# Longer load runs for k and v, 32-row products, and fewer whole-batch stores in a fused attention and spectral-mixing kernel

## The chip, the cores and the metric

One core of one Trainium2 chip. In the profile lines PE is the tensor engine (PEld its weight loads), DVE the vector engine, ACT the scalar engine, POOL the engine that issues the loads; PSUM is where this kernel's matmuls put their results. The metric is the device time of one execution in microseconds (us); lower is better. The kernel before has a median of 425.81 us (4 runs with the first measurement).

## The reference, cut to what matters

```python
# q, k, v: (8 batches, 8 heads, 576 rows, 64), float32
q_p, k_p = phi(q), phi(k)                       # phi(x) = elu(x) + 1
kv  = einsum('bhsd,bhse->bhde', k_p, v)         # per head: 64 x 64, summed over the 576 rows
z   = sum(k_p, axis=2)
x   = einsum('bhsd,bhde->bhse', q_p, kv) / (einsum('bhsd,bhd->bhs', q_p, z) + 1e-6)
# then, on x as (8, 576, 512): rfft over the rows, 64 modes, each times its own complex
# 512 x 512 weight (w_r, w_i: 134 MB in float32), irfft, u = x + y, out = u + relu(u @ w_ch)
```

The sum over s in `kv` does not care in which order the rows stand, as long as k and v have the same order. The change uses that.

## The kernel before

k and v of one batch are loaded so that a partition holds 9 consecutive rows (2,304 bytes of HBM, 1,152 bytes once cast to 16 bits). A head then fills 64 partitions. q has 18 rows to a partition.

```python
rows_in = src[b].rearrange("h s d -> (h s) d").rearrange(
    "(hp r j) d -> r hp (j d)", r=128, j=2 * NJ if nm == "q" else NJ)      # NJ = 9
...
shape = [128, 2, 2 * NJ * Dh] if nm == "q" else [128, NHP, NJ * Dh]
t = sA.tile(shape, F16, tag=f"{nm}16", bufs=2, name=f"{nm}16_{b}")
pin(nc.gpsimd.dma_start(out=t, in_=rows_in))
```

The products of k and v contract 64 rows; the two halves of the array (h2) alternate. Their sum is copied out by ACT (`kv`). Multiplied with q it gives the numerators of x, `num` below:

```python
def sum_kv(b):
    kv_ps = psA.tile([128, 2, 512], F32, tag="big", bufs=3, name=f"kvp{b}")
    for hpp in range(2):
        for j in range(NJ):
            for h2 in range(2):
                nc.tensor.matmul(kv_ps[:, h2, hpp*130 : hpp*130+130],
                                 phi["k", b][HALVES[h2], hpp, j]..., vp[HALVES[h2], hpp::2, j, 0:65], ...)
    # ... two ACT copies of 64 x 260 into kv_all[b]
```

Per batch the attention phase then runs, in this order (cut):

```python
turn_q(b, 0); turn_q(b, 1); sum_kv(b)      # tiles of tag "big", 3 buffers
features(b + 1)                            # DVE
exps(b + 2)                                # ACT: 4 passes
for jj in range(5):
    form_x(b, jj)                          # numerators `num`: one tile "big" each; jj = 4 is the tail
    if b > 1 and jj == 1: place_x(b - 2)   # `xp`: one tile "big", copied out by DVE and ACT into xt_c
    ...                                    # transforms of batch b - 1
```

`turn_q` transposes q (`qTp`), and `place_x` lays a batch's transformed rows out for the mode products (`xp`, copied out as `xt_c`).

Then 32 pairs of modes stream their weights (`w`, two transfers of 1 MB written per pair, two resident buffers), and at the end the output is stored. A batch in `QUADS` is stored whole (8 KB runs); the others in halves (4 KB runs):

```python
QUADS = (2, 4, 5, 6)
...
if t0 < B * NJJ and t0 // NJJ in QUADS:
    if t0 % NJJ:
        store(t0 - 2, NJJ)
    return
store(t0, 2)
```

## Time and profile before

| | before |
|---|---|
| span of the profiled execution | 422.9 us |
| load queue busy, from the packet records | 5.2 to 389.5 us |
| first products of the first mode pair | 113.9 us |
| last store issued / last store packet ends | 415.6 / 421.5 us |

From the page (busy time; then the 40 slices of the span in tenths; then packets by size):

```profile
PE 279.6 (66%) x3426; PEld 153.2 (36%) x3426; DVE 215.4 (51%) x446; ACT 161.7 (38%) x253; POOL 56.5 (13%) x99
...
DMA  9999999999999999999999999999999999996797
...
DMA packets 20227, 93.20 MB, mean 220 GB/s; under 512 B 2016, under 2 KB 11104, under 8 KB 15520
```

No compute engine is over 66% busy, and the DMA engines are full from the first slice to the thirty-sixth. The kernel is bound by its load stream. Compute matters in only two ways: if it is so late that the load queue runs dry, and after the last weight.

The store phase, by stretches (busy us of each engine, then granted clock, DMA share, GB/s):

```profile
396.00:400.00 4.00, 4.00 (x22) 1.22 (x21) 3.70 (x4) 3.38 (x8) 0.00 (x0) 1.00 1.00 383
400.00:404.00 4.00, 4.00 (x27) 1.11 (x27) 3.92 (x4) 3.46 (x7) 0.00 (x0) 1.00 0.79 321
404.00:408.00 4.00, 4.00 (x22) 0.82 (x20) 4.00 (x4) 3.47 (x8) 0.00 (x0) 1.00 0.99 388
408.00:412.00 4.00, 4.00 (x25) 1.17 (x24) 3.97 (x5) 3.63 (x7) 0.00 (x0) 1.00 1.04 431
```

The DMA share falls to 0.79 in one stretch: in the packet records fewer than 12 of 16 engines have a packet from 400.96 to 402.01 us. The stores wait there for the whole of batch 2.

The first mode pair, in order of time:

```profile
113.94 1.95 PE L442 MATMUL P<-w,xt_c 64*32 64x512 bf16 x32 [1.40 <-ACT xt_c L350]
```

### The profile page before, as it was taken

What the parts mean: (1) busy time and instruction counts of PE and PEld (TensorE: products, weight loads), DVE (VectorE), ACT (ScalarE), POOL (GpSimd) and SP (SyncE); (2) the same over time, 40 slices, a digit from 0 to 9 for tenths busy, and PEclk for the clock granted to TensorE, in tenths of its full rate; (3) what the DMA queues carried; (4) which work ended last, traced back from release to release, by engine and by line L of the source; (5) the groups of instructions that cost most, each with busy time, mean ns of one, the idle gap of its engine ahead of it and who ended that gap; (6) DMA issues with size and microseconds to landing.
All of it is one profiled execution on the core that took longest, in us unless ns stands there. A gap on an engine that the chain in (4) does not pass through costs nothing.

```text
span 422.9 us, 7976 instructions
## 1 busy us (share of the span) xinstructions
PE 279.6 (66%) x3426; PEld 153.2 (36%) x3426; DVE 215.4 (51%) x446; ACT 161.7 (38%) x253; POOL 56.5 (13%) x99
## 2 busy tenths in 40 slices
PE   1358387788717645344344768878798886989991
PEld 0246366666402322222122333334243333465320
DVE  4599488886202453354444434454264333423892
ACT  4688578754201102000000234444254351331881
POOL 4222124210000111111011111110110001130000
PEclk9999778869855555555555598999799896899997
DMA  9999999999999999999999999999999999996797
GB/s 217 210 208 215 207 220 202 224 209 222 221 215 219 207 215 217 222 211 217 218 212 217 217 220 214 215 216 215 214 219 220 215 212 219 223 201 126 248 409 287
DMA packets 20227, 93.20 MB, mean 220 GB/s; under 512 B 2016, under 2 KB 11104, under 8 KB 15520
## 3 DMA queue, kind: packets, MB, share of 16 engines
q0 software_dynamic: 16512, 81.47, 94.0%
q1 hardware_dynamic: 3680, 11.22, 7.0%
q8 instruction: 27, 0.44, 0.4%
q14 instruction: 8, 0.07, 0.0%
HBM read 163.93 MB, written 9.44 MB: 410 GB/s over the span
## 4 chain that ended last, share of the span: by engine, by line
DMA 63%; PE 22%; DVE 4%; ACT 3%; issue 2%; POOL 2%; DVEq 0%; POOLq 0%; ACTq 0%
DMA w<-in_moe_w_i_dram 48%; DMA pick_sb<-row_pick 8%; PE P L442 7%; DMA k<-in_k_dram 7%; PE acc L736 3%; PE acc L775 2%; PE zl L425 2%; ACT ke L213 2%; POOL w L119 1%; PE eps L677 1%; DVE ys L452 1%; PE ya L654 1%; PE yt L460 1%; PE xTp L667 1%; PE z L699 1%
## 5 line engine op out<-in xcount | busy, mean ns | idle before, releaser
L442 PE MATMUL P<-w,xt_c 64*32 64x512 bf16 (+2 forms) x1000 | 50.2, 531 | 59.7 <-DMA w<-in_moe_w_i_dram 58.3
L452 DVE CAST ys<-P 128x512 f16<-128x512 f32 x32 | 22.1, 692 | 122.2 <-PE P L442 122.2
L454 ACT CAST ys<-P 128x512 f16<-128x512 f32 x31 | 18.1, 585 | 154.1 <-PE P L442 154.1
L119 POOL DMA_DIRECT2D w<-in_moe_w_r_dram x31 | 16.6, 534 | 246.2 <-PE P L442 96.4
L442 PEld LDWEIGHTS <-xt_c 64*32 64x32 bf16 (+2 forms) x1000 | 16.7, 127 | 79.8 <-DMA w<-in_moe_w_i_dram 44.6
L165 PEld LDWEIGHTS <-qT 64*128 64x128 f16 (+1 forms) x640 | 23.0, 123 | 49.8 <-issue 31.0
L677 PE MATMUL eps<-wch,xTw 128*128 128x512 f16 x144 | 40.2, 406 | 0.0
L165 PE MATMUL num<-kv,qT 64*128 64x65 f16 (+1 forms) x320 | 13.7, 209 | 25.4 <-ACT xt_c L350 12.0
L658 DVE TENSOR_TENSOR x_main<-ya,x_main 128x512 f32<-128x512 f32 x32 | 22.0, 689 | 13.4 <-PE ya L654 13.2
L660 ACT CAST x16w<-x_main 128x512 f16<-128x512 f32 x32 | 19.8, 618 | 23.4 <-DVE x_main L658 22.3
L165 PE MATMUL nw<-kv,qT 64*128 64x65 f16 (+1 forms) x320 | 19.0, 240 | 9.5 <-DVE x_tail L621 4.3
L685 ACT CAST E<-eps 128x512 f16<-128x512 f32 (+1 forms) x40 | 21.2, 540 | 8.5 <-PE eps L677 8.4
L299 DVE TENSOR_TENSOR x<-num,rd 128x512 f16<-128x512 f32 x32 | 22.1, 692 | 1.1
L242 PE MATMUL qTp<-id,qe 128*128 128x128 f16 x144 | 16.1, 301 | 9.9 <-DVE qe L226 9.4
L460 PE MATMUL yt<-pick_sb,ys 128*128 128x16 f16 x252 | 11.7, 174 | 16.3 <-DMA pick_sb<-row_pick 9.6
L213 ACT ACTIVATE qe<-q 128x1152 f16<-128x1152 f16 (+1 forms) x16 | 17.9, 1157 | 10.4 <-DMA q<-in_q_dram 6.5
L249 ACT COPY qT<-qTp 128x1152 f16<-128x1152 f16 x16 | 19.6, 1287 | 0.7 <-PE qTp L242 0.2
L425 PE MATMUL zl<-wch,id 128*128 128x512 f16 x72 | 19.6, 408 | 0.0
L213 ACT ACTIVATE ke<-k 128x1152 f16<-128x1152 f16 x16 | 17.7, 1152 | 4.9 <-DMA k<-in_k_dram 4.9
L460 PEld LDWEIGHTS <-ys 128*128 128x128 f16 x252 | 9.7, 102 | 26.4 <-DVE ys L452 15.0
L785 ACT ACTIVATE acc<-acc 128x512 f32<-128x512 f32 x34 | 18.1, 582 | 2.4 <-PE acc L736 1.6
L242 PEld LDWEIGHTS <-qe 128*128 128x128 f16 x144 | 13.8, 140 | 11.0 <-DVE qe L226 9.8
(113 smaller groups left out, 468.6 us busy)
## 6 DMA issues: line engine op xcount, KB each, us to landing
w<-in_moe_w_r_dram POOLq DMA_DIRECT2D x31, 1024.0 KB, 12.5
w<-in_moe_w_i_dram POOLq DMA_DIRECT2D x31, 1024.0 KB, 17.0
k<-in_k_dram POOLq DMA_DIRECT2D x8, 576.0 KB, 12.8
v<-in_v_dram POOLq DMA_DIRECT2D x8, 576.0 KB, 14.8
out_dram<-x_main SPq DMA_DIRECT2D x4, 1024.0 KB, 4.9
q<-in_q_dram POOLq DMA_DIRECT2D x7, 576.0 KB, 12.9
out_dram<-x_main SPq DMA_DIRECT2D x6, 512.0 KB, 4.6
q<-in_q_dram SPq DMA_DIRECT2D x2, 576.0 KB, 4.3
```

What stands on the lines that cost most here:

```text
L119: nc.gpsimd.dma_start(out=w_in[p][half::2], in_=two.rearrange("g (r dc) e -> (g r) dc e", dc=NDW))
L165: mm = nc.tensor.matmul(num[hpo][orow, c0 : c0 + 65], qT[rows, hpp, h2, cols], kv_sb[rows, hpp, h2, :])
L213: pin(nc.scalar.activation(out=ev[:, c], in_=heads(nm, b, c), func=AF.Exp))
L242: nc.tensor.transpose(qT_ps[:, j], phi["q", b][:, c, j].rearrange("p o d -> p (o d)"), id16,)
L299: nc.vector.tensor_tensor(out=dst.rearrange("p (o c d) -> p o c d", o=2, c=4), in0=nv[:, :, :, 0:64], in1=rden.unsqueeze(3).broadcast_to([ ...
L425: pin(nc.tensor.matmul(last_ps[0], id16, wch16[:, 0, :]))
L442: nc.tensor.matmul(P[c : c + n, :], xt_cols(dc, kk, n), w[rows, dc, :], start=(dc < NDC), stop=(dc >= n_dc - NDC), tile_position=(rows.sta ...
L452: pin(nc.vector.tensor_copy(out=st, in_=P))
L460: nc.tensor.matmul(yt_ps[:, ec, kk % 8, :], st[:, ec * 128 : ec * 128 + 128], pick_sb)
L658: pin(nc.vector.tensor_tensor(out=x, in0=acc, in1=x, op=ALU.add))
L677: nc.tensor.matmul(e_ps, xT[:, c, :], wch16[:, c, :], start=(c == 0), stop=(c == NDC - 1))
L685: pin(nc.scalar.copy(out=dst, in_=e_ps[:, cols]))
```

## The change

Its intent: k and v in runs of 18 rows, so half as many packets, each twice as large. A head then fills only 32 partitions, so its products contract 32 rows, and there are twice as many of them. Besides, only batches 5 and 6 are stored whole.

```diff
-                "(hp r j) d -> r hp (j d)", r=128, j=2 * NJ if nm == "q" else NJ
+                "(hp r j) d -> r hp (j d)", r=128, j=2 * NJ
...
-        kv_ps = psA.tile([128, 2, 512], F32, tag="big", bufs=3, name=f"kvp{b}")
-        for hpp in range(2):
-            for j in range(NJ):
+        for pair in range(2):
+            kv_ps = psA.tile([128, 2, 512], F32, tag="big", bufs=3, name=f"kvp{b}_{pair}")
+            for j in range(2 * NJ):
                 for h2 in range(2):
+                    r0 = 64 * pair + 32 * h2
                     pin(
                         nc.tensor.matmul(
-                            kv_ps[:, h2, hpp * 130 : hpp * 130 + 130],
-                            phi["k", b][HALVES[h2], hpp, j].rearrange("p o d -> p (o d)"),
-                            vp[HALVES[h2], hpp::2, j, 0:65],
+                            kv_ps[:, h2, 0:130],
+                            phi["k", b][r0 : r0 + 32, j // NJ, j % NJ].rearrange("p o d -> p (o d)"),
+                            vp[r0 : r0 + 32, :, j, 0:65],
...
+                            tile_position=(r0, 0),
...              # the two ACT copies of 64 x 260 become four of 64 x 130
-    QUADS = (2, 4, 5, 6)
+    QUADS = (5, 6)
```

More of the change, by code (lines that the diff above doesn't have):

```diff
@@ L141 @@
     n_pre, n_keep = W_PRE, W_KEEP
-    vp = sA.tile([128, NHP, NJ, 66], F16, name="vpad")
+    vp = sA.tile([128, 2, 2 * NJ, 66], F16, name="vpad")
     nc.vector.memset(vp[:, :, :, 64:66], 1.0)
@@ L190, in load @@
                 continue
-            shape = [128, 2, 2 * NJ * Dh] if nm == "q" else [128, NHP, NJ * Dh]
-            t = sA.tile(shape, F16, tag=f"{nm}16", bufs=2, name=f"{nm}16_{b}")
+            t = sA.tile([128, 2, 2 * NJ * Dh], F16, tag=f"{nm}16", bufs=2, name=f"{nm}16_{b}")
             pin(nc.gpsimd.dma_start(out=t, in_=rows_in))
@@ L198, in heads @@
             return raw[nm, b, c].rearrange("p o (j d) -> p o j d", d=Dh)
-        if nm == "q":
-            return raw[nm, b].rearrange("p o (c j d) -> p c o j d", c=2, d=Dh)[:, c]
-        return raw[nm, b].rearrange("p (o c) (j d) -> p c o j d", o=2, d=Dh)[:, c]
+        return raw[nm, b].rearrange("p o (c j d) -> p c o j d", c=2, d=Dh)[:, c]
     def flat(nm, b):
@@ L254, in sum_kv @@
     def sum_kv(b):
-        kv_ps = psA.tile([128, 2, 512], F32, tag="big", bufs=3, name=f"kvp{b}")
-        for hpp in range(2):
-            for j in range(NJ):
+        for pair in range(2):
+            kv_ps = psA.tile([128, 2, 512], F32, tag="big", bufs=3, name=f"kvp{b}_{pair}")
+            for j in range(2 * NJ):
                 for h2 in range(2):
+                    r0 = 64 * pair + 32 * h2
                     pin(
                         nc.tensor.matmul(
-                            kv_ps[:, h2, hpp * 130 : hpp * 130 + 130],
-                            phi["k", b][HALVES[h2], hpp, j].rearrange("p o d -> p (o d)"),
-                            vp[HALVES[h2], hpp::2, j, 0:65],
+                            kv_ps[:, h2, 0:130],
+                            phi["k", b][r0 : r0 + 32, j // NJ, j % NJ].rearrange("p o d -> p (o d)"),
+                            vp[r0 : r0 + 32, :, j, 0:65],
                             start=(j == 0),
-                            stop=(j == NJ - 1),
-                        )
-                    )
-        for hpo in range(2):
-            rows = HALVES[hpo]
-            pin(
-                nc.scalar.copy(
-                    out=kv_all[b][rows],
-                    in_=kv_ps[rows, :, 0:260].rearrange("p t (c o n) -> p c t o n", c=2, o=2)[
-                        :, :, :, hpo, :
-                    ],
+                            stop=(j == 2 * NJ - 1),
+                            tile_position=(r0, 0),
+                        )
+                    )
+            for hpo in range(2):
+                rows = HALVES[hpo]
+                pin(
+                    nc.scalar.copy(
+                        out=kv_all[b][rows, pair], in_=kv_ps[rows, :, hpo * 65 : hpo * 65 + 65]
+                    )
                 )
-            )
     def form_x(b, jj):
```

## The prediction

> **What bounds the kernel now.** The DMA stream into the core. On the page the 16 DMA engines are 90% or more busy in 38 of 40 slices; in the packet records the software queue runs from 5.2 us to 389 us with no real gap, and only then do the stores start. So a saving counts only if it makes a packet cheaper or the store tail shorter; a loss counts only if it lets the load queue run dry.
>
> **What changes.**
> 1. k and v packets of 1152 B (written side) become 2304 B like q's. One takes 107 ns against 192, but packets overlap, so I use landing-to-landing times: k plus v take 5.68 us per batch, q 2.79. Gain 5.68 - 2 x 2.79 = 0.10 us per batch, about 0.85 us in all.
> 2. The k-times-v products double: 36 to 72 matmuls per batch, still 130 columns wide, contracting 32 rows instead of 64. Loop order leaves two row groups alternating, as before, so I expect the same start-to-start time per matmul: 52 ns at half clock, 29 at full clock (both in the records). The Trainium skill, "TensorE: Matmul & The Clock Gate", section "LDWEIGHTS", says a 32-row weight load takes as long as a 128-row one; halving the rows buys nothing. Extra PE time 1.0 to 1.9 us per batch; the clock usually rises during this product, so about 1.2.
> 3. ACT copies: 2 of 64x260 (370 ns) become 4 of 64x130, estimated 275 ns from 392 ns at 256 columns and 585 at 512. Two hide under the second pair's matmuls: about 0.2 us less after the last matmul.
> 4. Batches 2 and 4 leave as 4 KB-run half-stores: 163 ns per 4 KB against 317 per 8 KB, 0.15 us lost. But the store stream has a hole of 0.9 us at 401-402 us, waiting for batch 2's whole store; the half-store fills it. About 0.5 us gained.
>
> **What is critical.** In the attention phase batches 4 to 6 come every 11.2 us (starts of the q transposes). The loop, from the timeline: kv copies, exps (4.4), xt_c copy, last num products, transform, q transposes (2.1), kv products (1.2 to 1.9). The kv products lie on it, so from batch 3 on it grows by about 1 us per batch (before that, delay is absorbed waiting for k's DMA): pair 0's products end about 4.5 us later. The load issue that waits for them (the sixth weight pair) goes out at 116.2, and its first packet moves at 122.5; a late, unqueued transfer needed 2.0 us from issue. Slack is thus 4.3 us, 3.4 after step 1. So the queue runs dry for about 1 us (0 to 4). The q load of batch 7 (4.0 us from issue to first packet) is the other near miss.
>
> Sum: 425.8 - 0.85 - 0.5 + 1.0 = 425.4. Range 423.6 to 428.2. Chances: faster by over 2% 0.01, within 0.97, slower 0.02.
>
> **What would show it.** k and v about 2.79 us each between landings; matmul spacing 29/52 ns, a kv product 2 to 3.7 us long; first mode-pair products at about 118.5 instead of 113.9; a gap of about 1 us in the load queue before the sixth weight pair; no store hole at 401; tail about 0.5 us shorter; other groups unchanged.
>
> **What would make it wrong.** 32-row tiles pairing worse than 64-row ones (100 ns each would add 4 us per batch and starve the queue by 10 us or more); the clock not rising during the products; or no starvation at all, which gives 424.4.

## More of the kernel before

What the tensor engine waited for in the attention phase, from the view of waits (total us, times, longest), its two largest:

```profile
PE num L165 <- ACT xt_c L350: 12.0, 6, 6.2
PE num L165 <- ACT kv L272: 11.9, 16, 6.0
...
```

And one of those six waits in order of time (start, us, engine, line, operation; in brackets the idle time before it and what ended it):

```profile
45.08 0.37 PE L165 MATMUL num<-kv,qT 64*128 64x65 f16 x8
...
52.19 0.43 PE L165 MATMUL num<-kv,qT 64*64 64x65 f16 x8 [6.22 <-ACT xt_c L350]
...
54.09 2.10 PE L242 MATMUL qTp<-id,qe 128*128 128x128 f16 x18
```

The tail numerators of batch 2 stand still for 6.2 us because they were given the PSUM buffer that `xp` had, and ACT gets to copy `xp` out only after its exponentials.

## The result, and the profile after

The first measurement gave 422.61 us (422.50 to 422.93, 4 runs) against 425.81 (424.87 to 425.96, 4 runs): ratio 0.9931, 95% interval 0.9913 to 0.9948. It lies below my range (423.6 to 428.2). A ratio is the mean time of one kernel's runs over that of the other's of the same rounds, so not quite the ratio of the medians that I quote. Executions over 1.5% slower than the fastest of the same kernel are left out of the means.

The two kernels were then timed again beside the experiments. Pooled:

| | runs | mean | median | lowest | highest | within 0.6 us of the lowest |
|---|---|---|---|---|---|---|
| before | 54 | 425.52 | 425.69 | 424.57 | 426.51 | 17 |
| after | 16 | 423.07 | 422.67 | 422.38 | 425.03 | 11 |

So the change is worth 2.4 us in the mean (give or take 0.4, 95%, from the scatter of the runs; the mean still lies below my range) and 2.2 us between the lowest runs. The 3.2 us between the first medians also contains luck: all four runs of the changed kernel fell near its lowest.

The same lines of the page:

```profile
PE 292.1 (69%) x3714; PEld 162.7 (39%) x3714; DVE 215.7 (51%) x446; ACT 163.5 (39%) x269; POOL 56.9 (14%) x99
...
DMA  8999999999999999999999999999999999997697
...
DMA packets 16421, 93.24 MB, mean 222 GB/s; under 512 B 2048, under 2 KB 2944, under 8 KB 11968
```

There are 8,160 fewer packets under 2 KB, and PE has 12.5 us more busy time. The products of k and v up to 115 us, before and after (busy us, mean ns of one):

```profile
L261 PE MATMUL kvp<-vpad,ke 64*128 64x130 f16 x288 | 14.3, 274 | 4.7 <-DVE vpad L232 3.0 <-ACT qT L249 1.8
L259 PE MATMUL kvp<-vpad,ke 32*128 32x130 f16 x576 | 24.3, 261 | 9.0 <-ACT qT L246 6.1 <-DVE vpad L229 2.8
```

The waits of PE in the attention phase:

```profile
PE kvp L259 <- ACT qT L246: 6.1, 2, 4.6
PE num L165 <- DVE x L295: 3.2, 5, 1.0
...
PE qTp L239 <- ACT xt_c L346: 1.4, 1, 1.4
...
PE num L165 <- ACT xt_c L346: 0.4, 2, 0.2
```

and batch 2 in order of time:

```profile
49.74 0.51 PE L165 MATMUL num<-kv,qT 64*128 64x65 f16 x8
...
50.84 0.31 PE L165 MATMUL num<-kv,qT 64*64 64x65 f16 x8
...
52.13 1.18 PE L239 MATMUL qTp<-id,qe 128*128 128x128 f16 x18
```

and the first mode pair:

```profile
112.21 1.94 PE L438 MATMUL P<-w,xt_c 64*32 64x512 bf16 x32 [1.40 <-ACT xt_c L346]
```

The 12.0 us of waiting of the numerators for `xt_c` have become 0.4, and batch 3's q transposes start 2.0 us earlier than before, although more work was done by then. In the built program one sees the reason: before, the tail numerators of batches 2 to 7 wait for an ACT semaphore; after, those of batches 2 to 5 do not, and the next batch's q transposes wait for it instead. The PSUM pool has dealt its three buffers out otherwise. Two things temper this. Other waits moved too: that of the numerators for `kv` (11.9 us) is gone from the view, since the first numerators now start while the second pair is still being copied, and that of the products for `qT` grew from 1.8 to 6.1. And the clock is not the reason: from 41 to 112 us it was at full rate for 44 us after and for 47 before.

The store phase, the same stretches:

```profile
396.00:400.00 4.00, 4.00 (x26) 1.29 (x24) 3.90 (x4) 3.36 (x7) 0.00 (x0) 1.00 0.99 389
400.00:404.00 4.00, 4.00 (x24) 0.97 (x22) 3.92 (x5) 3.60 (x8) 0.00 (x0) 1.00 1.01 401
404.00:408.00 4.00, 4.00 (x22) 0.93 (x22) 4.00 (x4) 3.59 (x8) 0.00 (x0) 1.00 1.03 395
408.00:412.00 4.00, 4.00 (x28) 1.14 (x24) 3.97 (x4) 3.47 (x8) 0.00 (x0) 1.00 0.95 389
```

The hole at 401 us is gone, and a smaller one (409.3 to 409.6 us in the packet records) has come, before batch 5's whole store.

Where the 2.2 us between the two profiles lie, from four points of time in the packet and instruction records:

| stretch | before | after | difference |
|---|---|---|---|
| start to end of the last weight packet | 389.48 | 388.68 | -0.80 |
| from there to the first store issued | 4.03 | 3.98 | -0.05 |
| first store issued to last store packet | 27.98 | 26.79 | -1.19 |
| from there to the end of the span | 1.43 | 1.24 | -0.19 |

### The profile page after: what moved, and what is told of

Read it like the earlier page. It is cut to its first block, busy times and chain, and to the rows that moved or that the text cites. A ratio compares the mean times of both kernels' runs of the same rounds, so it can differ in the third digit from the quotient of the medians.

```text
span 420.7 us, 8570 instructions
## 1 busy us (share of the span) xinstructions
PE 292.1 (69%) x3714; PEld 162.7 (39%) x3714; DVE 215.7 (51%) x446; ACT 163.5 (39%) x269; POOL 56.9 (14%) x99
## 4 chain that ended last, share of the span: by engine, by line
DMA 64%; PE 22%; DVE 6%; issue 2%; POOL 2%; ACT 2%; DVEq 0%; POOLq 0%; ACTq 0%
DMA w<-in_moe_w_i_dram 51%; DMA pick_sb<-row_pick 8%; PE P L438 7%; DMA k<-in_k_dram 5%; PE acc L732 3%; PE acc L771 2%; PE kvp L259 2%; POOL w L119 2%; PE zl L421 1%; PE eps L673 1%; ACT ke L210 1%; DVE ys L448 1%; DVE x L295 1%; PE ya L650 1%; PE yt L456 1%
## 5 line engine op out<-in xcount | busy, mean ns | idle before, releaser
L259 PE MATMUL kvp<-vpad,ke 32*128 32x130 f16 x576 | 24.3, 261 | 9.0 <-ACT qT L246 6.1
L259 PEld LDWEIGHTS <-ke 32*128 32x128 f16 x576 | 22.2, 115 | 10.7 <-issue 8.2
L239 PE MATMUL qTp<-id,qe 128*128 128x128 f16 x144 | 14.1, 277 | 11.3 <-DVE qe L223 9.4
L165 PE MATMUL num<-kv,qT 64*128 64x65 f16 (+1 forms) x320 | 16.4, 218 | 5.5 <-DVE x L295 3.2
## 6 DMA issues: line engine op xcount, KB each, us to landing
v<-in_v_dram POOLq DMA_DIRECT2D x8, 576.0 KB, 14.5
```

The source lines that it names most:

```text
L165: mm = nc.tensor.matmul(num[hpo][orow, c0 : c0 + 65], qT[rows, hpp, h2, cols], kv_sb[rows, hpp, h2, :])
L259: nc.tensor.matmul(kv_ps[:, h2, 0:130], phi["k", b][r0 : r0 + 32, j // NJ, j % NJ].rearrange("p o d -> p (o d)"), vp[r0 : r0 + 32, :, j, 0 ...
```

## The experiments

Four questions: how the gain splits between loads and stores; whether the doubled products cost anything; why they did not delay the first mode pair; and why either kernel varies by up to 2 us. "P0" is the start of the first mode pair's products. P0 scatters: 113.9 and 114.4 us in the two profiles of the kernel before, 111.9 to 114.0 in three of the changed one. All kernels gave correct results except half_products, which is wrong on purpose.

### The kernel before against itself (before_again)

No edit. 

> The kernel before, unchanged, timed against itself. Ratio 1.000 within 0.002. It also tests whether the kernel before has two levels (about 424.8 and 425.9 us, as its earlier runs show): if so, its runs split again, and its profile shows where the 1 us lies. Theory L (the clock's rise falls differently from run to run, and a late load issue lets the load queue run dry now and then): a gap in the load queue in the slower runs. Rival: no gap; the packets are just a little slower.

Measured: 425.62 us median (424.84 to 426.51, 6 runs), ratio 1.0004 (0.9989 to 1.0018). The spread is there again, but its profile (425.18 us) has no gap in the load queue: between 6 and 377 us the 16 engines together lost at most 0.2 us. So a dry queue, my theory L, is not shown to be the reason for the spread; nor is the rival, since nothing but 0.3 us at the start of the stream differs. It took other runs to find it (below).

### Loads and products without the stores (loads_only)

```diff
 (the changed kernel)
-    QUADS = (5, 6)
+    QUADS = (2, 4, 5, 6)
```

> The changed loads and products, but the stores as before (whole-batch stores for 2, 4, 5, 6). Theory A (two separate gains): load packets give 0.85 to 0.9 us and no starvation, so 424.8 us if the median of before is 425.8 (ratio 0.998). Theory B (most of the 3 us comes from the loads and the warmer tensor clock): 423.3 us or less (ratio 0.994).

Measured: 423.88 us (423.59 to 424.92), ratio 0.9970 (0.9955 to 0.9984), so 1.3 us gained. In its profile the last weight packet ends at 388.63 us against 389.48 and the hole is back. The packet records give the mechanism cleanly. Loads that follow each other on the queue end one after another; k plus v took 5.68 us per batch before and take 5.58 now (2.79 each, like q). The last load of the attention phase ends at 82.3 us in the mean of five profiles with 9-row runs and at 81.4 us in five with 18-row runs: 0.9 us, which is what eight batches of 0.10 us give. The load stream is theory A's; the time lies between A (424.8) and B (423.3), nearer B. So some 0.4 us of this run's gain are not the loads; the run with the products made twice, below, hints at where they come from.

### The stores alone (stores_only)

```diff
 (the kernel before)
-    QUADS = (2, 4, 5, 6)
+    QUADS = (5, 6)
```

> Only the store list changed to batches 5 and 6. Theory A: the hole of 1.05 us in the store stream goes, a new one of 0.35 us comes, the rest of the stores go a little faster: 1.2 us gained, 424.6 us (ratio 0.997), and time from last store issue to last store packet falls from 5.9 to 4.7 us. Theory B: 0.5 us or less (ratio 0.999).

Measured: 424.95 us (424.15 to 425.57), ratio 0.9987 (0.9974 to 0.9999): about 0.6 us. The hole is gone (401 GB/s from 401 to 402 us, against 107 before). The time from last store issue to last store packet is 5.40 us in this profile. Over all profiles with the old list it is 5.66 to 6.11 us (mean 5.92, six profiles), with the new one 4.68 to 5.40 (mean 4.95, eight profiles). So by their tail the stores are worth about 1.0 us, more than my 0.5, with a scatter of 0.3 us either way; the time of this run alone would be theory B's (0.999). This profile also showed the first sign of the spread's cause: it has its last products 0.5 us late, after a stretch in which the clock was down. The stretches 360 to 367 and 367 to 374 us, in this kernel:

```profile
360.00:367.00 7.00, 6.48 (x70) 3.07 (x69) 3.36 (x6) 2.31 (x4) 1.06 (x2) 0.98 1.01 215
367.00:374.00 7.00, 7.00 (x53) 2.03 (x52) 1.27 (x3) 1.85 (x5) 0.00 (x0) 0.53 1.03 220
```

and in the kernel before, where the clock stayed up:

```profile
360.00:367.00 7.00, 6.48 (x67) 2.89 (x65) 2.59 (x5) 1.76 (x3) 1.06 (x2) 0.85 1.03 220
367.00:374.00 7.00, 7.00 (x78) 4.05 (x79) 3.16 (x6) 3.51 (x6) 1.88 (x4) 1.00 1.04 220
```

The column after the engines is the granted clock: 0.53 against 1.00, and 53 matmuls against 78 in the same 7 us.

### The products twice, in the kernel before (products_twice)

```diff
-        for hpp in range(2):
+        for hpp in (0, 1, 0, 1):
```

> The kernel before with every k-times-v product made twice with 64-row groups (the second overwrites the first; the result stays right): the added tensor work of the change without its loads or stores. My prediction's step said the first mode-pair products would come 4.5 us later and the load queue would starve by up to 1 us (ratio 1.000 to 1.005). Theory C (the longer dense stretch brings the clock up, so the added work pays for itself): first mode-pair products at 113 to 114.5 us as in the kernel before, no gap in the load queue, ratio 1.000 within 0.001, mean spacing of a product's matmuls under 47 ns in at least four of eight batches.

Measured: 424.66 us, all five runs from 424.56 to 424.73, ratio 0.9980 (0.9968 to 0.9992). P0 was at 111.9 us, 2 us before that of the kernel before, with 288 matmuls more. So the added work costs nothing; even my theory C had not expected P0 to come earlier. It even gains: the interval of the ratio ends below 1, and all five runs lie within 0.2 us of the lowest of the kernel before, as only 9 of its 54 do. The traced spans are equal (422.9 us), so what it gains is that no run was long; I come back to this under what stays open. The clock was up for 60 of the 71 us from 41 to 112 us, against 47 before, and five of eight products had a mean spacing of 29 ns. At this point I took the clock for the cause. But the same profile has the waits of the numerators for `xt_c` down from 12.0 to 0.6 us, so it mixes two causes.

### The changed kernel again (after_again, after_third)

No edit. 

> The changed kernel again, on the same chip as the next three. If the first result holds: 422.6 us, ratio 0.993, runs within 0.5 us of each other. If the 3 us were partly luck of the earlier chip (the parts gave only 1.3 and 0.6 us): ratio 0.995 to 0.996.

Measured: 422.97 us (422.57 to 425.03), ratio 0.9952 (0.9932 to 0.9972): the second of the two cases that I had set out, part of the first 3 us was luck.

> The changed kernel a third time. Pooled so far: 423.1 us against 425.5 (0.9944). Expected 422.6 to 423.4, ratio 0.993 to 0.996; its slower runs owe it to the clock at the end, so two of six over 423.5.

Measured: 422.66 us (422.38 to 424.08), ratio 0.9944 (0.9925 to 0.9963), two of six runs over 423.5, as expected.

### Half of the products left out (half_products)

```diff
 (the changed kernel; wrong result on purpose)
-            for j in range(2 * NJ):
+            for j in range(NJ):
...
-                            stop=(j == 2 * NJ - 1),
+                            stop=(j == NJ - 1),
```

> The changed kernel with every second row's product left out (wrong result on purpose): 36 matmuls per batch as in the kernel before, loads and stores as in the changed one. Theory C (the doubled products pay for themselves by the clock, and only the load queue's packets and the stores gain): the same time as the changed kernel within 0.5 us, first mode-pair products at 112 to 114 us. Rival D (the denser attention phase itself shortens the kernel by 0.9 us, as the run with products made twice hinted, 0.998): 0.9 us slower than the changed kernel, with runs spread over 1.5 us as in the kernel before.

Measured: 423.40 us (423.19 to 424.73), ratio 0.9961 (0.9943 to 0.9979), 0.4 us above the changed kernel of the same job, which is within the noise; the spread, 1.5 us, says little beside the changed kernel's own in that job (2.5), so rival D is neither borne out nor excluded. With half the products P0 came at 115.7 us, later than in any profile of the changed kernel (111.9 to 114.0) and outside theory C's 112 to 114. Here the numerators wait again for `xt_c`:

```profile
PE num L165 <- ACT xt_c L346: 7.4, 5, 4.6
```

and the clock was up for only 24 us of 71. So P0 moves by several us in the direction opposite to the tensor work, and the time of the kernel does not follow it.

### Less filler at the end, in the kernel before (before_less_fill)

Fillers are matmuls whose result nobody reads, put in to keep the clock up; `FILL` gives their number after each mode pair.

```diff
-    FILL = {**{p: 5 for p in range(18, 27)}, 27: 8, 28: 2, 29: 7, 30: 7}
+    FILL = {**{p: 5 for p in range(18, 27)}, 27: 8, 28: 2, 29: 7, 30: 2}
```

> The kernel before with 2 instead of 7 filler matmuls after the last full mode pair: 1.1 us less tensor work between the landing of pair 30's weights and the last product. Theory E (the kernel before spreads over 424.7 to 426.2 because its tensor engine is late, by an amount that depends on where the clock fell, at the end of the weight stream): mean 424.8, spread under 0.5 us, ratio 0.998. Rival: no change (ratio 1.000), or slower because the clock falls without the filler.

Measured: 424.94 us (424.68 to 425.82), ratio 0.9992 (0.9978 to 1.0006). A spread of 1.1 us remains. Theory E in this form is not borne out: the tensor engine's lateness at the end is not cured by taking 1.1 us of filler away.

### No whole-batch stores (no_quads)

```diff
 (the changed kernel)
-    QUADS = (5, 6)
+    QUADS = ()
```

> The changed kernel with no whole-batch stores at all (all stores of two row tiles, 4 KB runs). If the gain of the store change is the hole alone, the last hole (0.35 us at 409 us) goes and 1 MB more in 4 KB runs costs 0.1 us or less: 0.0 to 0.3 us faster than the changed kernel. If longer runs matter as the list suggests, 0.2 us or more slower.

Measured: 424.16 us (422.98 to 424.90), ratio 0.9967 (0.9950 to 0.9984), which would be slower than the changed kernel. Its profile (424.52 us) tells why not to trust that: first store issued to last store packet is 27.11 us, in line with the changed kernel's 26.74 to 27.09, and the hole at 409 us is gone. What is long is the time from the last weight to the first store, 5.20 us against 3.98, behind a half-clock stretch from 366.6 to 373.5 us. The store list beyond (5, 6) makes no difference that these runs can resolve.

### What the spread is

Put together, the 16 profiles other than late_40 and late_70 split without exception by one thing:

| half-clock stretch between 366 and 393 us | profiles | last weight packet to first store issued |
|---|---|---|
| none | 12 | 3.96 to 4.05 us |
| one | 4 (stores_only, no_quads, after_again, before_no_wait) | 4.46, 5.20, 5.07, 5.15 us |

The Trainium skill, "TensorE: Matmul & The Clock Gate", section "What's actually happening", says that the clock passes either all pulses or half of them, by how busy the engine has been in a free-running window of about 3.4 us. The traces agree: granted clocks are 1.0 or 0.5 only, and the stretches last 3.41 us or a multiple (6.83, 10.24). Where these windows fall differs from run to run (in the three profiles of the changed kernel the clock first rises at 50.5, 41.9 and 49.8 us), so by this reading the same kernel drops or keeps the clock at its end by chance. For the changed kernel and the variants the split is plain. For the kernel before itself it is carried over: 34 of its 54 runs took 425.48 us or more, but its two traced runs (424.79 and 425.18 us) have no such stretch.

### A late first mode pair (late_40, late_70)

```diff
 (the changed kernel, ahead of the first mode pair; n = 40 and n = 70)
+    late_ps = psB.tile([128, D], F32, tag="bank", bufs=4, name="late")
+    for _ in range(n):
+        pin(nc.tensor.matmul(late_ps, id16, fwd_sb.rearrange("p a m -> p (a m)")[:, 0:D]))
```

> The changed kernel with 40 idle matmuls (about 8.6 us) ahead of the first mode pair, so its products end later. Traces so far: at 114.2 us and at 117.7 us (half_products) nothing was lost. My prediction put the last moment at which the sixth weight pair's issue may leave without loss at about 119.6 us (slack 3.4 us). Here the first pair should end at 120 to 121 us. If that slack was right: a gap of 1 to 2 us in the load queue near 121 us and the kernel 1 to 2 us slower than the changed one (424 to 425 us). If the slack is larger: no gap, 422.5 to 423.2 us.

Measured: P0 at 122.5 us, later than planned; 425.16 us (423.59 to 428.99, 4 runs), ratio 1.0004. The profile shows what a late issue does. When the sixth pair's weights were issued:

```profile
123.91 0.52 POOL L119 DMA_DIRECT2D w<-in_moe_w_r_dram  x1 [31.60 <-PE P L438]
```

and how full the DMA engines were (share and GB/s are the last two columns):

```profile
118.00:122.00 4.00, 4.00 (x20) 1.82 (x19) 0.00 (x0) 0.00 (x0) 0.00 (x0) 1.00 0.95 180
122.00:126.00 4.00, 2.66 (x75) 1.28 (x73) 0.69 (x1) 0.58 (x1) 1.06 (x2) 1.00 0.74 98
```

From 122.3 us the queue is dry; the first packet of the new transfer moves at 125.14 us, 1.23 us after the issue began. The engines lost 2.4 us in all there. So an issue up to about 122.3 - 1.2 = 121 us should lose nothing: an estimate, between the issue at 120.0 us that lost nothing (forced_wait, below) and this one.

> The same with 70 idle matmuls (about 15 us): first pair ends at 126 to 128 us. The load queue must then run dry for 6 to 8 us and the kernel must be slower by the same amount (429 to 431 us). If it is not, the load stream does not bound the kernel as I say.

Measured: 433.05 us (428.52 to 434.06, 4 runs), ratio 1.0155 (1.0114 to 1.0197). In the profiled run (428.52 us) the issue left at 126.6 us and the engines lost 5.1 us. I had expected 6 to 8 us lost and 429 to 431 us. Lateness beyond the deadline is paid, and the load stream is the bound. Why the three runs without a trace took 4.5 us more than the traced one is open.

### Four row groups in turn (four_way)

```diff
 (the changed kernel)
-        for pair in range(2):
-            kv_ps = psA.tile(...)
-            for j in range(2 * NJ):
+        kv_ps = [psA.tile(...) for pair in range(2)]
+        for j in range(2 * NJ):
+            for pair in range(2):
                 for h2 in range(2):
...              # the four ACT copies follow after both pairs
```

> The changed kernel with the four row groups taken in turn (two PSUM tiles at once), the same 72 matmuls. If groups of 32 rows run side by side, spacing falls to about 15 ns at full clock and 27 at half, so the products take 1 to 2 us as in the kernel before. Theory C: with the shorter dense stretch the clock is lower again, the first mode pair comes no earlier than in the changed kernel (112.2 us), and the time is the same within 0.5 us, since the load stream is never late.

Measured: 422.87 us (422.62 to 423.77), ratio 0.9940 (0.9923 to 0.9957). Four matmuls start every 58 ns at full clock and every 108 ns at half clock, so about 14.5 and 27 ns each: groups of 32 rows do run side by side, twice as fast as in the changed kernel's order, where only two groups alternate (29 and 54 ns). P0 came at 111.5 us, within 0.4 us of the earliest of the changed kernel, so nothing for or against theory C. The time is that of the changed kernel, since P0 does not count.

### Fillers moved to where the clock drops (warm_folds, best)

```diff
 (the changed kernel)
-    FILL = {... 29: 7, 30: 7}
+    FILL = {... 29: 3, 30: 3}
...  # in fold_lead
+        keep_warm(1)
```

> The changed kernel with one filler matmul in each of the eight early folds near 363 to 370 us, and four fewer after each of the last two full pairs. Theory E (the runs 1 to 2 us above the floor are those in which the clock fell to half between 366 and 374 us or near 390 us): at most one run of six over 423.3 us, mean 422.8 or less, ratio 0.993 to 0.994; no half-clock stretch between 360 and 415 us in its trace. Rival: spread as before (three of six over 423.2), mean 423.2.

Measured: 422.93 us (422.52 to 423.24, 6 runs), ratio 0.9938 (0.9923 to 0.9952), mean 422.91, no run over 423.3 and no half-clock stretch near the end. That is what theory E forecast, save for the mean (422.8 or less). But it is weak: 12 of 16 runs of the changed kernel are under 423.3 us anyway, so six in a row come by chance about one time in six, and the mean is only 0.16 us below that of the changed kernel, which is not a difference.

> The changed kernel with the fillers moved as in warm_folds and one whole-batch store only (batch 6). Expected: runs within 0.7 us of each other, mean 422.7 us, at most 0.4 us faster than the changed kernel, ratio 0.993. If the store list still matters the hole of 0.35 us near 409 us goes; if not, no difference to warm_folds (422.9).

(Same edit, and `QUADS = (6,)`.) Measured: 423.18 us (422.94 to 423.78), ratio 0.9948 (0.9932 to 0.9964). The mean, 423.3, missed the expected 422.7: no gain over warm_folds. No version that I tried beats the changed kernel clearly.

### Clock or PSUM buffer (forced_wait, before_no_wait)

In forced_wait the tail numerators are put into `xp`'s own tile, so that they must wait for ACT's copy of it as in the kernel before:

```diff
 (the changed kernel, in form_x)
-        num = psA.tile([128, 2, 512], F32, tag="big", bufs=3, name=f"num{b}_{jj}")
+        if tail and b > 1:
+            num = xp_ps[b - 2].rearrange("p i c t m -> p (i c t m)").rearrange("p (o n) -> p o n", o=2)
+        else:
+            num = psA.tile([128, 2, 512], F32, tag="big", bufs=3, name=f"num{b}_{jj}")
...  # place_x keeps its tile in xp_ps[b]
```

> The changed kernel, but the last numerators of batches 2 to 7 go into the placing product's own PSUM tile, so that they must wait for its scalar copy as in the kernel before; 72 matmuls per batch as in the changed kernel. Theory F (the vanished PSUM wait is what hid the doubled products): the first pair's products start at 117 to 119 us, about what I had predicted (118.5), instead of 112.2. Theory C (the clock alone): 112 to 113 us. Either way no gap in the load queue (the issue may leave as late as about 121 us) and the changed kernel's time, 422.6 to 423.4 us.

Measured: P0 at 117.7 us, as theory F said, 0.8 us before what I had predicted for the changed kernel. The enforced wait is 6.2 us, not 12.0, and the clock was up for only 32 us of 71 against 44, so part of the delay may be the clock's. Its waits and its first mode pair:

```profile
PE xp L165 <- ACT xt_c L350: 6.2, 6, 3.5
```

```profile
117.67 1.94 PE L442 MATMUL P<-w,xt_c 64*32 64x512 bf16 x32 [1.40 <-ACT xt_c L350]
```

And yet the time is 422.71 us (422.42 to 423.27), ratio 0.9935 (0.9919 to 0.9951), the changed kernel's. The sixth pair's weights were issued at 120.0 us, and the DMA engines stayed full:

```profile
119.97 0.52 POOL L119 DMA_DIRECT2D w<-in_moe_w_r_dram  x1 [27.78 <-PE P L442]
...
118.00:122.00 4.00, 1.61 (x32) 0.54 (x17) 0.69 (x1) 0.59 (x1) 1.06 (x2) 0.50 1.05 204
122.00:126.00 4.00, 1.40 (x32) 0.79 (x39) 0.00 (x0) 0.00 (x0) 0.00 (x0) 0.50 1.13 228
```

In before_no_wait the wait is taken out of the kernel before, by giving ACT's copy to DVE:

```diff
 (the kernel before, in place_x)
-        pin(nc.scalar.copy(out=xt_v[:, h:NDW, :, b, :], in_=psf[:, h:NDW]))
+        pin(nc.vector.tensor_copy(out=xt_v[:, h:NDW, :, b, :], in_=psf[:, h:NDW]))
```

> The kernel before with both copies out of the placing product's tile on the vector engine, so that the last numerators no longer wait behind the scalar engine's exponentials; 36 matmuls per batch. Theory F: the first pair starts at 108 to 111 us instead of 114, the wait of the last numerators falls from 12 us to under 3. Theory C: 113 us or later. The time stays that of the kernel before, 425.5 us within 0.6 (ratio 0.999 to 1.001), since the load stream was never late.

Measured: P0 at 110.1 us; the time is 425.88 us (424.86 to 426.01), ratio 1.0005 (0.9989 to 1.0020).

```profile
PE num L165 <- ACT kv L272: 17.2, 16, 6.0
...
PE num L165 <- DVE xt_c L350: 0.7, 3, 0.3
```

```profile
110.11 1.11 PE L442 MATMUL P<-w,xt_c 64*32 64x512 bf16 x32 [1.38 <-DVE xt_c L350]
```

So the wait was worth about 4 us of P0 in the kernel before and nothing of its time; of the 12 us, 5.3 came back as waiting for `kv`. The clock is ruled out here: it was up for 48 us of 71, against 47. The run shows that the wait for the PSUM buffer moves P0. Together with forced_wait it shows that the first pair may end anywhere from 111.2 to 119.6 us and leave the time alone.

## Why the prediction was right or wrong, point by point

- **The bound: right.** The load stream, then the store stream. late_70 shows that starving it is paid. (The page has 37 slices of 90% or more, not 38.)
- **Step 1, cheaper load packets: right.** Predicted 0.85 us; the load stream ends 0.8 us earlier in the two profiles and 0.9 us in the mean of five against five. Each k or v takes 2.79 us, as said.
- **Step 2, the cost of the products: right in size on the tensor engine.** Spacings are 29 and 54 ns with two groups alternating, and PE has 10.0 us more busy time in this group (14.3 to 24.3). The statement that I drew on, that a 32-row weight load takes as long as a larger one, agrees with the records: at full clock a weight load of these products takes 91 ns (median) with 32 rows and 93 with 64.
- **Step 3, the copies: right.** A copy of 64x130 takes 262 ns (275 estimated), and from the start of a batch's last product to that of `xp` it is 1.39 us against 1.53 (medians of six batches).
- **Step 4, the stores: right mechanism, mis-sized.** I put down "About 0.5 us gained"; it is 1.0 us in the mean of the profiles (5.92 to 4.95 us from last issue to last packet), 1.2 us in the first profile. The holes alone give 1.05 - 0.35 = 0.7; the 0.15 us that I charged for shorter runs is not seen.
- **The step that failed: "So the queue runs dry for about 1 us (0 to 4)."** It ran dry in no profile of the changed kernel. The prediction names this case itself: "no starvation at all, which gives 424.4". Two terms of the step were wrong. First, "pair 0's products end about 4.5 us later": they came 1.7 us earlier, since the pool dealt out its PSUM buffers otherwise and 12.0 us of waiting fell to 0.4. That the wait is worth microseconds of P0 is shown by before_no_wait (4 us, same clock). forced_wait, with a wait for that buffer back, has P0 at 117.7 us, so a delay of about the size that I forecast does come with it, though its lower clock has a part in it. Second, "Slack is thus 4.3 us": late_40 puts the latest harmless issue at about 121 us in the changed kernel, 6.5 us after its own issue at 114.5. In the kernel before, whose stream is 0.9 us later, that makes about 122 us, or 5.7 us of slack. I had taken 2.0 us from issue to first packet, from another transfer, where 1.2 was measured for the weights. With this slack alone the term is zero, as forced_wait shows: issue at 120.0 us, nothing lost.
- **A term that I left out: the level from which I subtracted.** I started from 425.8, the median of the kernel before, of which 17 of 54 runs lie near 424.6. The four first runs of the changed kernel all lay near its own lowest. The sum with the measured terms, -0.9 for the loads and -1.0 to -1.4 for the stores and the end of the span, gives -1.9 to -2.3, which is the difference of the lowest runs (2.2) and, within the noise, of the means (2.4). The remaining 0.8 us of the first 3.2 is luck: three of the four first runs of the kernel before were long, and none of the changed kernel's. That the clock makes the long runs is read from the variants' profiles, not shown by an experiment that sets it.

What stays open: loads_only and stores_only add to about 1.8 us, against 2.4 for both; their intervals allow it. There is also a rival that I did not test apart. In four profiles of the kernel before and its variants the products of the last full pair start 8.9 us before the last weight lands, in the changed kernel 9.5, so the kernel before has less room for a clock that drops. This goes with the number of products and not with the loads: products_twice, with the old loads, has 9.5 us and no long run; half_products, with the new loads, has 8.9 us. So the doubled products themselves may make long runs rarer, and with that be a part of the gain in the mean. The packet records offer a reason: with 36 products per batch a 16 KB packet of the queue called "instruction" starts about 2 us before that pair's weights have landed (378.47 and 380.50 us in the kernel before), with 72 it starts some 4 us before (375.25 and 379.11 in the changed one). That this packet makes the difference was not tested.

## What to carry to other kernels

When a load queue bounds a kernel, price a change at the queue: per-packet cost from one landing to the next, and for everything else only whether the latest issue still comes before the queue is dry; measure that deadline with a delay put in on purpose before charging for it. Compare the waits in the built programs before and after, not only the code: a change in one product can make a buffer pool deal its buffers out otherwise and move a wait of 12 us that the diff does not mention (here worth 4 us of P0, and nothing of the time). And with differences of half a per cent, find out first between which levels a kernel's runs jump and why, before subtracting from a median.

## What the Trainium skill lacked or had wrong

- "TensorE: Matmul & The Clock Gate", section "Wait — 56ns, not 53.3ns?", gives about 25 ns as the least time from start to start of matmuls. With four 32-row groups in turn the records here show four starts in 58 ns at full clock, 14.5 ns each (four_way). (Elsewhere the page does describe row groups that run side by side; only this sentence lacks the exception.)
- The same page, section "The mechanism", says that matmuls are strictly first in, first out. In the changed kernel the 16 matmuls about the change from one pair of row groups to the next start at 14.5 ns each in some batches, as if the second pair's began while the first pair's were still queued; the records do not name the row groups, so this is an inference.
- "DMA: Bandwidth & Descriptors", section "Latency and other measured facts", gives about 1 us to the first byte of a software-built transfer. The one case here with a dry queue agrees: 1.23 us from the start of the issue (late_40). The page does not say how long a queue stays fed after its last issue, which is what sets the deadline: in the changed kernel the next issue could have come about 6.5 us later than it did.
- The same page, section "Measured (HBM→SBUF, 128 partitions, SWDGE, issued from GpSimd)", rates single transfers and asks for 1 MiB and more. Transfers of 576 KB queued back to back reach 212 GB/s written here against 216 for those of 1 MB, so between these two sizes it matters little once the queue is full.
- No page says that a tile pool's choice of PSUM buffers can change with an unrelated product; here it moved 12.0 us of waits to 0.4.
